# Linear attention and a four-expert block: neighbouring chunks share up products

## The chip, the cores and the metric

The kernel runs on one core of one Trainium2 chip. A core has five engines that work side by side: TensorE (matrix multiplication, "PE" in the profile, its weight loads "PEld"), VectorE ("DVE"), ScalarE ("ACT"), GpSimd ("POOL") and SyncE ("SP", which here only issues DMAs). TensorE writes to the PSUM banks; DVE and ACT carry results from there to SBUF. The metric is the device time of one execution in microseconds (us), the median of several runs.

## The reference

Two blocks follow each other. The first is a linear attention: for each of 8 batches and 8 heads (576 tokens, head size 64) it forms `kv = k^T v`, multiplies `q` by it, and divides every row of 64 numbers by its root mean square. Joined over the heads that gives `x` with 4608 rows of 512 numbers. The second block sends every row through all four experts and adds the results:

```python
kv = np.einsum('bhsd,bhse->bhde', k, v)
out = np.einsum('bhsd,bhde->bhse', q, kv)
x = out / sqrt(mean(out*out, -1) + 1e-6) * g_norm      # -> (4608, 512)
p = domain_probs / (domain_probs.sum(-1, keepdims=True) + 1e-09)
for e in range(4):
    out += p[:, e:e+1] * (np.maximum(x @ w1[e], 0.0) @ w2[e])   # w1: 512x1024, w2: 1024x512
```

Everything is float32.

## The kernel before, in words

**Chunks and steps.** The rows of `x` are cut into 9 chunks of 512 tokens: one for each batch (its first 512 tokens), and a ninth made of the 64 left-over tokens of all 8 batches. A step is one chunk through one expert: expert 0 takes all nine chunks, then expert 1, and so on, 36 steps in all. During expert 0 the attention of the next batch runs beside the products of the current chunk. `CHUNKS` (L2117) holds the order of the chunks in each expert; in expert 1, chunk 0 comes fifth.

**Seven products for eight, twice.** The product `x @ w1[e]` ("up") and the product `h @ w2[e]` ("down") are not done as plain blocks. A product of 2 x 2 blocks is done with seven block products in place of eight (Strassen's scheme in Winograd's form), at the price of additions of blocks. This is done at two levels: seven outer products, numbered 1 to 7 in the code (`OUTER`), each of which is again done as seven inner products (`ORDER`). So "up" has 49 inner products for a chunk. An inner product multiplies a 128 x 256 piece of the weights with 128 tokens; it is issued as four matmul calls (`halves_of`, L585, two halves of 64 columns for each of two pieces of 128 units), and the profile shows eight matmul instructions for each: the weights are stationary, 128 tokens move through. The weights' forms are made once for an expert, the tokens' forms once for a chunk; expert 0 writes the latter to DRAM (`keep`, `x_kept`), and later experts read them back (`x_again`, L1476) into five buffers of kind `xf`, one for each outer product, 512 KB each.

**Up, `up` (L1514).** The inner products of one outer product go to three PSUM banks. Products 1, 6, 7 and 4 add up in the first one; after product 1, ACT copies the bank into the second bank as a seed (L1563, `u<-u`), on which product 2 adds; products 5 and 3 add up in the third. After products 6 and 7, ACT copies the state of the first bank to a small SBUF buffer (`snap`). Two of the four quarters of the result are ACT copies of a bank (L1563, `big<-u`), and two are DVE additions of a bank and a `snap` (L1571). So one outer product costs five ACT passes and two DVE passes over 128 x 256 numbers. Then the outer results are added up (`combine`, L608, on DVE or POOL), and ACT applies the ReLU (L1527).

**Down, `down_deep` (L1819).** Its seven outer products are done in groups of up to two. The results are added in SBUF (L1944); ACT multiplies them by the token's probability into two accumulator buffers of the kind `big` (`result`, L1681; `merge`, L1716), and `send` (L1732) sends them out: in expert 0 as plain stores by SP, in later experts as adding DMAs by POOL (L1740), 128 rows of 2 KB in one DMA. The last step adds in SBUF instead. The first seven chunks of expert 0 use `down_first`, in which three products are done in one level with 256 moving numbers.

**Norm's factors.** For each batch of expert 0 the sums of squares come from TensorE; ACT and DVE make the inverse roots, SP stores them in a small DRAM tile `roots` (L1297) and reads them back spread over the partitions (`spread` L1303, `spread_left` L1311), in rows of 512 and 128 bytes; DVE multiplies (L1322).

**What sets the order.** Nothing is ordered by hand. Every operation is given to a planner (`class Plan`, L44) with a key (its place in steps), a cost on each engine that may do it, its reads and its writes. The planner plays the execution and gives each engine a fixed order, picking the operation with the earliest due time among those that are ready, or for SP the first by key. It also gives out the buffers. `DEALS` (L72) lists for some steps numbers of random draws that shift due times there.

Of the kernel before, what the change touches and what calls it, by code (L numbers as in the profile page):

```python
# [43 lines left out]
class Plan:  # L44
# [25 lines left out]
    FIRST = "SP",  # L70
    BLOCK, ASKED, BEGUN, IDLE, FULL = 256, 30, 66, 20, 45.0
    DEALS = {  # L72
# [4 lines left out]
    }  # L77
    SHARED, AHEAD, INORDER = ("big",), 0.3, ("xf",)

# [375 lines left out]
def kernel(  # L455
# [65 lines left out]

    BANKS = {"u1": 2, "u2": 2, "db": 2, "ab": 2}
    SHAPE = {
        "big": (31, 2 * NT), "w1y": (7, 768), "xa": (1, 4 * NT), "xb": (1, 4 * NT),
        "w2e": (1, 2 * NT), "snap": (5, HN),
        "ss": (2, H), "rt": (2, 2 * H),
    }
    slots = {
# [5 lines left out]
    for kind, n in BANKS.items():  # L534
# [14 lines left out]
    slots["small"] = [small_home[:, 2 * QW:2 * QW + NT]]  # L549
    slots["small2"] = [small_home[:, 2 * QW + NT:2 * QW + 3 * NT]]  # L550
    slots["w2y"] = [w2y_home[:, i, :] for i in range(3)]
    halved = slots["db"]
# [3 lines left out]
    later = [  # L556
        ((kind,), "xf", [slots[kind][0][:, i * 2 * NT:(i + 1) * 2 * NT] for i in range(n)])
        for kind, n in (("xa", 2), ("xb", 2), ("w2e", 1))
    ] + [
        (("raw",), "db", halved),  # L560
        (("kv", "kvbd"), "w2y", [kv_flat[:, i * 768:(i + 1) * 768] for i in range(4)]),
# [8 lines left out]
        for c in range(NCH) for m in ("h0", "h1", 1, 2, 3, 4, 5, 6, 7)  # L570
    }
    roots = {
        b: dram.tile([D, P + 32], F32, tag=f"roots{b}", name=f"roots{b}") for b in range(1, B)
    }

    plan = Plan()
# [544 lines left out]
    def attention(b, key, span, rem):  # L1121
# [160 lines left out]
        def invert(eng):  # L1282
# [11 lines left out]
        sent, kept_roots = Buf(None, f"root{b}"), roots[b]  # L1294
        plan.add(
            when, SPC,
            lambda eng: nc.sync.dma_start(out=kept_roots[:], in_=both[0].ap[0:P:2, 0:wide]),  # L1297
            reads=both[:1], writes=[sent], kb=41, lands=2.6,
        )
        for s, (qt, tokens, mine) in enumerate(done):  # L1300
            xh = x_halves(b)[s]

            def spread(eng, xh=xh, s=s):  # L1303
                rows = kept_roots[:].rearrange("(n i s r) t -> r s i n t", i=2, s=2, r=2)
                for r in range(2):
                    nc.sync.dma_start(
                        out=xh.ap[r * D:(r + 1) * D, :].rearrange("p (n t) -> p n t", t=P),
                        in_=rows[r, s, 0, :, 0:P].unsqueeze(0).to_broadcast([D, 8, P]))

            def spread_left(eng, s=s, mine=mine):  # L1310
                rows = kept_roots[:].rearrange("(j i s r) t -> r s i j t", i=4, s=2, r=2)  # L1311
                for r in range(2):
                    nc.sync.dma_start(
                        out=xs.ap[r * D:(r + 1) * D, mine].rearrange("p (j t) -> p j t", j=NR),
                        in_=rows[r, s, 0, :, P:wide].unsqueeze(0).to_broadcast([D, NR, R]))
# [4 lines left out]
            plan.add(  # L1320
                when, dve(2 * NT),
                lambda eng, xh=xh, qt=qt: nc.vector.scalar_tensor_tensor(  # L1322
                    out=two(xh.ap[:]), in0=tokens(qt.ap, False), scalar=gcol[:], in1=two(xh.ap[:]),
                    op0=ALU.mult, op1=ALU.mult),
                reads=[qt, xh], writes=[xh], port=True,
            )
# [149 lines left out]
    def x_again(c, key, step):  # L1476
        views = {}
        for j, m in enumerate(OUTER):
            f = Buf("xf", f"xl{c}_{m}")
            if m in (1, 2, 3):  # L1480
                half = "h0" if m == 1 else "h1"
                cols = slice(HN if m == 3 else 0, NT if m == 3 else HN)
                load(
                    key + j * step, f, lambda f=f: two(f.ap[:, 0:NT]),
                    two(x_kept[c, half][:])[:, :, cols], 256, reads=[kept[c, half]],
                )
                load(
                    key + j * step, f, lambda f=f: f.ap[:, NT:], x_kept[c, m][:], 256,
                    reads=[kept[c, m]],
                )  # L1490
            else:
                load(
                    key + j * step, f, lambda f=f: f.ap[:], x_kept[c, m][:], 512,
                    reads=[kept[c, m]],
                )
            views[m] = {
                n: (f, lambda f=f, at=at: f.ap[:, at * P:(at + 1) * P])
                for n, at in ((1, 0), (2, 2), (3, 3), (5, 4), (7, 5), (6, 6), (4, 7))
            }
        return views  # L1500


    hidden = {}
    summed = {}
# [9 lines left out]
    def up(s, e, views):  # L1514
# [16 lines left out]
        for i, m in enumerate(OUTER):  # L1531
# [64 lines left out]
            if m == 2:  # L1596
                add(key, unit(1), made[1], made[2])
                relu(key, h[1])
            elif m == 6:
                add(key, made[1], made[1], made[6])  # L1600
            elif m == 5:
                add(key, made[6], made[1], made[5])
            elif m == 3:
                add(key, unit(21), made[6], made[3])
                relu(key, h[21])
                add(key, unit(7), h[1], h[21], ALU.subtract)
            elif m == 7:
                add(key, made[1], made[1], made[7])
                add(key, unit(4), made[1], made[5], where=dve)
                relu(key, h[4])  # L1610
                add(key, unit(5), h[21], h[4], where=dve)
                add(key, unit(6), h[5], h[1], ALU.subtract, dve)
            elif m == 4:
                add(key, unit(2), made[1], made[4])
                relu(key, h[2])
                add(key, unit(3), h[2], h[6], ALU.subtract)
        hidden[s] = h

    def up_plain(s, e, c, key, span):
# [199 lines left out]
    def down_deep(s, e, c, groups=((1, 6), (7, 5), (4, 2), (3,)), base=None, h=None, merge=None, send=None, ends=False, sink=None):  # L1819

        mixed = h is not None
        if not mixed:
            h = hidden.pop(s)
            base = s + 1.2
            merge, send = result(s, e, c, base)
        prods, half = {}, {}

        for i, group in enumerate(groups):
# [132 lines left out]
            elif mixed:  # L1964
                out_(3, 0, 1)
                if not ends:
                    out_(5, 0, 1)
                    out_(5, 1, 1)
                    send(key, 2)
                    send(key, 3)  # L1970
                    send(key, 0)
                    send(key, 1)
            elif i == 0:
                add(6, 1, 6)
            elif i == 1:
                add(7, 6, 7)
                add(6, 6, 5)
                add(5, 7, 5)
                out_(5, 1, 1)
            elif i == 2:  # L1980
                add(4, 7, 4)
                out_(4, 1, 0)
                send(key, 2)
                send(key, 3)
                add(2, 1, 2)
                out_(2, 0, 0)
            else:
                add(3, 6, 3)
                out_(3, 0, 1)
                send(key, 0)  # L1990
                send(key, 1)

    def down_first(s, e, c):

# [119 lines left out]
    inner = {0: weights_2(0, 0.25, 0.04, 8.2)}  # L2114
    inner[0]((1, 7, 6, 5), 0.5)
    norm_probs(0.10)
    CHUNKS = {e: list(range(NCH)) for e in range(E)}  # L2117
    CHUNKS[1].insert(4, CHUNKS[1].pop(0))
    CHUNKS[E - 1][-2:] = NCH - 1, NCH - 2
    for e in range(E):  # L2120
        for i in range(NCH):
# [7 lines left out]
            if s + 1 < E * NCH:  # L2129
# [3 lines left out]
                    x_views[s + 1] = x_forms(c + 1, s + 0.7)  # L2133
                else:
                    again = CHUNKS[(s + 1) // NCH][(s + 1) % NCH]
                    made = x_first if (s + 1) // NCH == 1 and again == 0 else x_again
                    x_views[s + 1] = made(again, s + (0.05 if e else 0.6), 0.13)
            if s:
# [73 lines left out]
```

## Time and profile before

| | before |
|---|---|
| median of 3 runs | 1631.18 us (1630.81 to 1631.45) |
| the profiled execution's own time | 1631.92 us |
| its span, first to last instruction | 1630.1 us |
| PE busy | 1622.5 us (100%) |
| DVE / ACT / POOL busy | 1337.2 / 986.9 / 612.9 us |
| matmul instructions | 29082 |
| clock granted to TensorE | 1.000 of full speed |

The span lies inside the time of the execution; the rest is start and end. "Busy" is the time in which an engine had at least one instruction in hand. For matmuls, which follow each other in a pipeline, it says little about speed; the distance between the starts of successive instructions says more. Under "idle before", a group of instructions has the time that its engine stood idle ahead of them, and what ended it.

### The profile page before, as it was taken

The numbers are of one execution on the slowest core, as the hardware profiler recorded it, in microseconds if no ns is written. First come the engines' busy times: TensorE is split into PE (matmuls) and PEld (weight loads), VectorE is DVE, ScalarE is ACT, GpSimd is POOL, SyncE is SP. The second block draws the span as 40 slices with busy tenths as digits, with TensorE's granted clock in tenths as the row PEclk, the third lists the DMA queues.
The fourth block names the chain that finished last, engine by engine and source line by source line (L and its number), as shares of the span: only waits on it lengthen the run. The fifth ranks groups of instructions, "written<-read, shape, count | busy, mean of one in ns | idle before, by whom it ended". The sixth has DMA issues, their size and how long they took to land.

```text
span 1630.1 us, 66925 instructions
## 1 busy us (share of the span) xinstructions
PE 1622.5 (100%) x29082; PEld 1564.6 (96%) x29082; DVE 1337.2 (82%) x2188; ACT 986.9 (61%) x2504; POOL 612.9 (38%) x597
## 2 busy tenths in 40 slices
PE   9999999999999999999999999999999999999999
PEld 5788999989999999999999999999999999999998
DVE  5788888889888888878988888887788987777776
ACT  4456655665566666666666666666566666566563
POOL 4233432323443443344344533332344443332232
PEclk9999999999999999999999999999999999999999
DMA  9877787855664435444676454444478544444442
GB/s 242 217 190 204 204 216 194 213 166 205 183 176 125 118 93 156 119 111 113 175 190 144 107 133 114 108 111 111 131 183 184 131 107 117 118 107 117 118 106 53
DMA packets 229312, 241.02 MB, mean 148 GB/s; under 512 B 101047, under 2 KB 172542, under 8 KB 229018
## 3 DMA queue, kind: packets, MB, share of 16 engines
q1 hardware_dynamic: 205402, 199.96, 40.9%
q0 software_dynamic: 23616, 36.78, 15.2%
q8 instruction: 228, 3.74, 1.0%
q14 instruction: 66, 0.54, 0.1%
HBM read 162.21 MB, written 74.47 MB: 145 GB/s over the span
## 4 chain that ended last, share of the span: by engine, by line
PE 98%; DVE 1%; DMA 1%; ACT 0%; issue 0%; SPq 0%; DVEq 0%; ACTq 0%
PE u L585 48%; PE db L585 31%; PE ab L585 16%; PE ab L1193 1%; PE ab L1218 0%; PE ab L1261 0%; PE ab L2156 0%; PE db L1218 0%; DVE big L608 0%; DMA kv<-in_v_dram 0%; DMA out_dram<-big 0%; SPq L2079 0%; PE u L997 0%; DMA small<-in_q_dram 0%; DVE small L608 0%
## 5 line engine op out<-in xcount | busy, mean ns | idle before, releaser
L608 DVE TENSOR_TENSOR big<-big,big 128x1024 f32<-128x1024 f32 (+1 forms) x612 | 547.6, 913 | 32.3 <-ACT big L1527 14.1
L585 PE MATMUL db<-big,big 128*64 128x128 f32 (+1 forms) x5464 | 397.1, 283 | 0.3 <-DVE big L608 0.3
L585 PEld LDWEIGHTS db<-big,big 128*64 128x64 f32 x5464 | 319.1, 137 | 16.7 <-issue 0.6
L1563 ACT ACTIVATE snap<-u 128x256 f32<-128x256 f32 x490 | 187.7, 383 | 178.3 <-PE u L585 156.5
L1571 DVE TENSOR_TENSOR big<-u,snap 128x256 f32<-128x256 f32 x450 | 189.0, 421 | 112.8 <-PE u L585 74.2
L608 POOL TENSOR_TENSOR big<-big,big 128x256 f32<-128x256 f32 (+1 forms) x149 | 165.4, 1111 | 229.6 <-DVE big L608 91.0
L1563 ACT ACTIVATE big<-u 128x256 f32<-128x256 f32 x450 | 172.8, 385 | 84.1 <-PE u L585 63.5
L585 PE MATMUL u<-xb,big 128*64 128x128 f32 x2880 | 212.4, 273 | 0.1
L585 PE MATMUL u<-xa,big 128*64 128x128 f32 x2784 | 205.2, 273 | 0.1
L608 POOL TENSOR_TENSOR big<-big 128x512 f32<-128x512 f32 (+1 forms) x94 | 111.4, 1186 | 235.7 <-DVE big L608 137.4
L1905 ACT ACTIVATE snap<-db 128x256 f32<-128x256 f32 (+1 forms) x268 | 95.3, 356 | 126.8 <-PE db L585 104.4
L585 PEld LDWEIGHTS u<-xb,big 128*64 128x64 f32 x2880 | 168.8, 137 | 2.2 <-issue 0.3
L585 PE MATMUL u<-xa,w1y 128*64 128x128 f32 x2232 | 165.8, 273 | 0.0
L585 PEld LDWEIGHTS u<-xa,big 128*64 128x64 f32 x2784 | 162.5, 137 | 2.2 <-issue 1.2
L585 PE MATMUL u<-xb,w1y 128*64 128x128 f32 x2208 | 164.2, 273 | 0.0
L1527 ACT ACTIVATE big<-big 128x1024 f32<-128x1024 f32 x133 | 139.9, 1054 | 11.0 <-DVE big L608 9.4
L1913 DVE TENSOR_TENSOR big<-ab,snap 128x256 f32<-128x256 f32 x186 | 78.4, 421 | 65.6 <-ACT snap L1905 39.0
L608 DVE TENSOR_TENSOR big<-big 128x512 f32<-128x512 f32 (+1 forms) x167 | 125.2, 756 | 7.6 <-POOL big L608 4.4
L585 PEld LDWEIGHTS u<-xa,w1y 128*64 128x64 f32 x2232 | 130.6, 137 | 0.7 <-DVE xb L608 0.4
L585 PEld LDWEIGHTS u<-xb,w1y 128*64 128x64 f32 x2208 | 129.1, 137 | 1.3 <-issue 0.4
L1740 POOL DMA_DIRECT2D out_dram<-big x124 | 108.0, 1155 | 32.5 <-ACT big L1716 18.0
L1563 ACT ACTIVATE u<-u 128x256 f32<-128x256 f32 x245 | 90.9, 371 | 38.7 <-PE u L585 28.1
(246 smaller groups left out, 2838.8 us busy)
## 6 DMA issues: line engine op xcount, KB each, us to landing
xb<-x SPq DMA_DIRECT2D x44, 512.0 KB, 3.6
xa<-x SPq DMA_DIRECT2D x40, 512.0 KB, 3.6
out_dram<-big POOLq DMA_DIRECT2D x76, 256.0 KB, 6.0
big<-in_moe_w_dram SPq DMA_DIRECT2D x27, 512.0 KB, 6.3
w2e<-x SPq DMA_DIRECT2D x20, 512.0 KB, 3.6
xa<-x_h SPq DMA_DIRECT2D x37, 256.0 KB, 3.5
x_h<-big SPq DMA_DIRECT2D x18, 512.0 KB, 4.9
x<-xb SPq DMA_DIRECT2D x18, 512.0 KB, 4.9
```

Of the source, the lines that this page charges most:

```text
L585: nc.tensor.matmul(out_[cols], lhsT=lhsT[:, cols], rhs=rhs, **kw)
L608: lambda eng: adder(eng).tensor_tensor(out=out_(), in0=a(), in1=b(), op=op),
L1193: nc.tensor.matmul(bank.ap[o * D:(o + 1) * D, r * D:(r + 1) * D], lhsT=ks[r], rhs=vs[r], start=(j == r == 0), stop=(j == len(sets[0]) - 1) ...
L1527: lambda eng: nc.scalar.activation(out=b.ap[:], in_=b.ap[:], func=ACT.Relu),
L1563: lambda eng: nc.scalar.activation(out=where(), in_=ps.ap[:, 0:HN], func=ACT.Copy),
L1571: lambda eng: nc.vector.tensor_tensor(out=block(whole, a, t), in0=src.ap[:, 0:HN], in1=add_.ap[:], op=ALU.add),
L1740: nc.gpsimd.dma_start(out=dst, in_=cell(i)[parts, :], accum_op=ALU.add)
L1905: lambda eng: nc.scalar.activation(out=where(), in_=group_of(ps.ap), func=ACT.Copy),
L1913: lambda eng: nc.vector.tensor_tensor(out=cell(tq, dq), in0=group_of(src.ap), in1=group_of(add_.ap), op=ALU.add,),
```

## The change

**Joint up products.** In experts 1 to 3, `up_shared` takes the place of `up`. Neighbouring chunks of an expert share three of their seven outer products, in turn 6, 7, 4 and 2, 3, 5: an inner product of those is issued once with 256 moving tokens, 128 of each chunk. Chunk 0 in expert 1 has no partner. `course` gives every outer product its place; 8 pairs of neighbours in experts 2 and 3 and 6 in expert 1 make 22 pairs. The five `xf` buffers become one tile (`x_home`), so that two of them can be read by one access pattern of two runs of 128; a joint outer product holds two of them, and `x_again` loads them at keys that `course` gives. A bank of a joint product holds 512 numbers for each partition. There is no seed: ACT copies the bank after products 1, 6 and 7 straight to the place of a result quarter, for each chunk, and DVE adds to that in place after products 2, 5 with 7, and 3. For each chunk of a joint outer product that makes four ACT passes and three DVE passes. Single outer products are evacuated as before. The ReLU and several sums are made in place.

**Down finished in place.** `down_whole` takes the place of the form of `down_deep` with accumulators (steps 7 to 34): ACT multiplies the results where they lie (`finish`), and each of the four results of 256 tokens x 256 columns is sent on its own, in rows of 1 KB. The groups of outer products alternate with the chunk (`DEEP`).

**Norm's factors.** The inverse roots are stored by two DMAs into two DRAM tiles, and read back by one DMA each in place of two, in rows of 4 KB and 512 bytes.

**Draws.** `DEALS` lists other draws, and for 35 of the 39 steps from -3 to 35; before for 21.

```diff
-        -3: (920, 388), -2: (494, 764), -1: (959, 295), 0: (983,), 3: (1126, 364), 4: (981, 960), 5:
...
+        -3: (920, 388), -2: (494, 764, 638), -1: (959, 295, 323), 0: (1187,), 1: (859,), 2: (321,),
...
+    x_home = pool.tile([P, 5, 2 * NT], F32, tag="x", name="x")
+    x_at = [x_home[:, i, :] for i in range(5)]
...
+    HEADS, ENDS = (2, 3, 5), (6, 7, 4)
+    MIDDLES = (1,), (1,)
+    DEEP = ((1, 6), (7, 5), (4, 2), (3,)), ((4, 5), (2, 1), (7, 6), (3,))
...
-            plan.add(when, {"SP": 1.2}, spread, reads=[sent], writes=[xh], kb=520, lands=6.2)
-            plan.add(when, {"SP": 1.28}, spread_left, reads=[sent], parts=[xs], kb=100, lands=6.0)
+            def spread(eng, i, to, s=s):
+                rows = roots[b][i][2 * s:2 * s + 2].rearrange("r n t -> r (n t)")
+                return nc.sync.dma_start(out=to, in_=rows.unsqueeze(1).to_broadcast([2, D, rows.shape[1]]))
...
+    def course(e):
+        uses, at, shared = [{} for _ in range(NCH)], 0.0, ()
+        for i, c in enumerate(CHUNKS[e]):
+            turn = i % 2
+            first, end = (ENDS, HEADS) if turn else (HEADS, ENDS)
+            beside = i + 1 < NCH and not (e == 1 and 0 in (c, CHUNKS[e][i + 1]))
...
+            for m in joint:
+                uses[i][m] = uses[i + 1][m] = at, 2
+                at += 2
...
+    def up_shared(s, e, i, uses, views, following):
...
+                    if n == 1:
+                        x = both[0][m][mm][1]()
+                    else:
+                        lo, hi = sorted(place(0)[0])
+                        col = both[0][m][mm][2] * P
+                        x = x_home[:, lo:hi + 1:hi - lo, col:col + P]
+                    for u in range(2):
+                        halves_of(
+                            ps.ap[:, u * n * P:(u + 1) * n * P], w[:, u * P:(u + 1) * P], rhs=x,
+                            start=((mm in (1, 5) or mm == 2 and n == 2) and u == 0), stop=True,
+                            skip_group_check=True,
+                        )
...
+                if joint:
+                    for o in range(2):
+                        if mm in (1, 6, 7):
+                            early(o, *{1: (0, 0), 6: (0, 1), 7: (1, 1)}[mm])
+                        if mm == 2:
+                            total(o, 0, 0, ps, None)
+                        elif mm == 7:
+                            total(o, 1, 1, bank[5], None)
+                        elif mm == 4:
+                            copy(o, wholes[o], lambda o=o, cell=cell: cell(o, 1, 0))
+                        elif mm == 3:
+                            total(o, 0, 1, ps, None)
+                    continue
...
+    def finish(s, e, c, q, th, dh, key, prods, half, whole):
...
+                    out=whole(q)[:, t * HN:(t + 1) * HN], in_=whole(q)[:, t * HN:(t + 1) * HN],
+                    func=ACT.Copy, scale=p_all[:, c * NR + i, e:e + 1]),
...
+    def down_whole(s, e, c, turn):
...
+                for parts, b, dst in where:
+                    src = two(whole(q))[parts, b, :]
+                    if e:
+                        nc.gpsimd.dma_start(out=dst, in_=src, accum_op=ALU.add)
+                    else:
+                        nc.sync.dma_start(out=dst, in_=src)
...
+            if e:
+                up_shared(s, e, i, uses[e], x_views.pop(s), x_views.get(s + 1))
             elif s:
                 up(s, e, x_views.pop(s))
...
-                down_deep(s, e, c)
+                down_whole(s, e, c, i % 2 if e else 0)
```

More of the change, by code (lines that the diff above doesn't have):

```diff
@@ L556 @@
     later = [
[L557 to L558 removed]
+        ((kind,), "xf", x_at[at:at + n]) for kind, at, n in (("xa", 0, 2), ("xb", 2, 2), ("w2e", 4, 1))
     ] + [
@@ L572 @@
     roots = {
-        b: dram.tile([D, P + 32], F32, tag=f"roots{b}", name=f"roots{b}") for b in range(1, B)
+        b: [
+            dram.tile([n, D // n, width], F32, tag=f"roots{b}_{n}", name=f"roots{b}_{n}")
+            for n, width in ((8, P), (16, 32))
+        ] for b in range(1, B)
     }
@@ L1293, in attention @@
             when, {"DVE": 0.57 + 0.0031 * wide}, invert, reads=[ss, both[0]], writes=both[:1], port=True)
[L1294 to L1299, printed above, removed]
+        sent = [Buf(None, f"root{b}_{i}") for i in range(2)]
+        for i, cols in enumerate((slice(0, P), slice(P, wide))):
+            plan.add(
+                when, SPC,
+                lambda eng, i=i, cols=cols: nc.sync.dma_start(
+                    out=roots[b][i][:].rearrange("m n t -> n m t"), in_=both[0].ap[0:P:2, cols]),
+                reads=both[:1], writes=[sent[i]], kb=(32, 8)[i], lands=2.6,
+            )
@@ L1500, in x_again @@
         return views
+    def course(e):
[4 more added lines that the diff above has]
+            beside = i + 1 < NCH and not (e == 1 and 0 in (c, CHUNKS[e][i + 1]))
+            todo = [m for m in OUTER if m not in shared] if not turn and not shared else [
+                m for m in first + MIDDLES[turn] + end if m not in shared]
+            joint = end[::-1] if turn else end
+            joint = joint if beside else ()
+            for m in todo:
+                if m not in joint:
+                    uses[i][m] = at, 1
+                    at += 1
+            for m in joint:
+                uses[i][m] = uses[i + 1][m] = at, 2
+                at += 2
+            shared = joint
+        return uses
     hidden = {}
@@ L1817, in down, with down_deep @@
             down_deep(s, e, c, ((4, 2), (3, 5)), base + 3 / 7, h, merge, send)
[L1819 to L1828, printed above, removed]
+    def down_deep(s, e, c, groups, base, h, merge=None, send=None, ends=False, sink=None, full=False):
+        mixed = not full
         prods, half = {}, {}
@@ L1978, in down_deep @@
                 add(5, 7, 5)
-                out_(5, 1, 1)
-            elif i == 2:
+                emit(5, 1, 1, key, prods, half, whole)
                 add(4, 7, 4)
[L1982 to L1991, printed above, removed]
+                emit(4, 1, 0, key, prods, half, whole)
+            elif i == 3:
+                add(1, 6, 3)
+                emit(1, 0, 1, key, prods, half, whole)
+        down_deep(s, e, c, groups, base, h, sink=sink, full=True)
+        for i, b in now.items():
+            summed[c, i] = b
     def down_first(s, e, c):
```

262 lines of the change are left out of this document (235 added, 27 removed), and 8 rows, old and new, of the table DEALS.

## The prediction

> **What bounds the kernel now.** I read the page first, then the busy times by stage, then the waits.
>
> ```profile
> span 1630.1 us, 66925 instructions
> PE 1622.5 (100%) x29082; PEld 1564.6 (96%) x29082; DVE 1337.2 (82%) x2188; ACT 986.9 (61%) x2504; POOL 612.9 (38%) x597
> PE 98%; DVE 1%; DMA 1%; ACT 0%; issue 0%; SPq 0%; DVEq 0%; ACTq 0%
> ```
>
> ```profile
> 20.00:470.00 450.00, 448.04 (x7642) 396.56 (x7642) 374.35 (x626) 262.76 (x671) 159.33 (x145) 1.00 0.71 195
> 470.00:860.00 390.00, 390.00 (x7142) 389.43 (x7140) 334.95 (x534) 245.87 (x617) 161.42 (x162) 1.00 0.55 140
> 860.00:1240.00 380.00, 380.00 (x6968) 380.00 (x6964) 317.07 (x506) 237.51 (x602) 147.29 (x143) 1.00 0.51 128
> 1240.00:1600.00 360.00, 360.00 (x6600) 359.90 (x6597) 284.62 (x459) 222.96 (x565) 131.14 (x125) 1.00 0.48 116
> ```
>
> The columns are the stretch, its length, the busy time of PE, PEld, DVE, ACT and POOL with instruction counts, the granted clock, the DMA share and GB/s. The chain of work that ended last is PE for 98%. The four stretches are about experts 0, 1, 2 and 3. A busy PE proves little, so I use the counts: 380.00 / 6968 = 54.5 ns for each matmul instruction in the third stretch, 360.00 / 6600 = 54.5 in the fourth, 390.00 / 7142 = 54.6 in the second. Is that the pace of back-to-back work? The timeline of PE says yes:
>
> ```profile
> 679.81 1.04 PE L585 MATMUL db<-w2y,big 128*64 128x128 f32 x16
> ...
> 699.46 0.61 PE L585 MATMUL u<-xa,big 128*64 128x128 f32 x8
> ```
>
> Between these two starts lie 360 instructions of 128 moving rows, the 16 of the first row among them: 19.65 us / 360 = 54.6 ns, or 0.4367 us for an inner product of eight. So experts 1 to 3 hold no stall that could be won back. There only fewer or cheaper matmuls shorten the run. All waits of PE that the profile names add up to 3.5 us:
>
> ```profile
> PE u L585 <- DMA small<-in_q_dram: 1.2, 1, 1.2
> PE ab L2156 <- DVE eps L2163: 1.0, 1, 1.0
> PE ab L1063 <- DVE big L928: 0.8, 1, 0.8
> PE db L585 <- DVE big L608: 0.3, 1, 0.3
> PE ab L1193 <- DMA out_dram<-big: 0.2, 1, 0.2
> ```
>
> **Joint products on PE.** 22 pairs of chunks x 3 outer x 7 inner products = 462 joint products, each eight instructions of 256 moving rows for sixteen of 128: 3696 matmuls fewer. Up in experts 1 to 3 has no 256-row matmul before; the nearest rows are those of the last step, with contiguous operands:
>
> ```profile
> 1610.98 1.90 PE L585 MATMUL u<-big,big 128*64 128x256 f32 x16
> 1612.70 1.04 PE L585 MATMUL db<-big,big 128*64 128x128 f32 x16
> ...
> 1614.89 1.90 PE L585 MATMUL u<-big,big 128*64 128x256 f32 x16
> 1616.61 0.61 PE L585 MATMUL db<-w2y,big 128*64 128x128 f32 x8
> ...
> 1618.36 1.90 PE L585 MATMUL db<-big,big 128*64 128x256 f32 x16
> 1620.09 0.61 PE L585 MATMUL db<-small,big 128*64 128x128 f32 x8
> ```
>
> From start to next start sixteen take 1.72, 1.72 and 1.73 us, so eight take 5.17 / 6 = 0.862 us. Two products of 128 rows take 2 x 0.4367 = 0.873. The gain is 0.011 us for a joint product; with two digits in each time it may be 0.008 to 0.015. The other bound is a longer stretch of 512-row matmuls at the start:
>
> ```profile
> 25.92 8.80 PE L585 MATMUL u<-big,big 128*64 128x512 f32 x40
> 34.65 1.14 PE L1085 MATMUL db<-kv,big 64*64 64x64 f32 x16
> ```
>
> That is 8.73 / 40 = 218 ns, exactly four times 54.6: by this row longer matmuls win nothing. It ends in a change of tile shape, which the joint products don't have, so I take 0.010, the lower side of the nearer rows. 462 x 0.010 = **-4.6 us**; the ends are 0 and 462 x 0.015 = -6.9. The moving operand now has two runs in two buffers, which no row shows; a price for it is what the end at 0 stands for.
>
> The Trainium skill ("TensorE: Matmul & The Clock Gate", section "Wait — 56ns, not 53.3ns?") gives each warm matmul its rows at 2.4 GHz and about 2.5 ns that don't depend on the rows. By it a joint product would save 8 x 2.5 = 20 ns, 9.2 us in all, an estimate from that page. The trace disagrees: its 54.5 ns lie under the 55.8 that the rule gives for 128 rows, so half the fixed cost at most is there to be saved.
>
> **What evacuates the joint products.** For each chunk of a joint outer product one ACT pass goes and one DVE pass comes.
>
> ```profile
> L1571 DVE TENSOR_TENSOR big<-u,snap 128x256 f32<-128x256 f32 x450 | 189.0, 421 | 112.8 <-PE u L585 74.2
> L1563 ACT ACTIVATE u<-u 128x256 f32<-128x256 f32 x245 | 90.9, 371 | 38.7 <-PE u L585 28.1
> ```
>
> 22 x 3 x 2 = 132 passes: DVE +132 x 0.421 = 55.6 us, ACT -132 x 0.371 = -49.0 us. By expert DVE gets 36, 48 and 48 passes, 15.2, 20.2 and 20.2 us: 335 + 15 of 390 is 90%, 317 + 20 of 380 is 89%, 285 + 20 of 360 is 85%. The largest idle time ahead of L1571 is time spent waiting for PE, so DVE runs ahead of its input there. The chain inside a bank relaxes for PE: before, product 6 waited for one ACT pass of 371 ns against a product of 437; now it waits for two passes, some 0.75 us, against a product of 0.862, with the down products of the step before between them as now. Cost on the path: 0, hidden under PE; if that cover goes, up to the whole 55.6, which is the slower rival below. ReLUs and sums keep their number and sizes.
>
> **x loads.** Their number stays; their places on SP move, and a joint product frees its two buffers together.
>
> ```profile
> SPq L614 <- PE u L585: 916.3, 192, 10.7
> xb<-x SPq DMA_DIRECT2D x44, 512.0 KB, 3.6
> ```
>
> SP already spends 916 us standing before a load until PE frees a buffer; behind it wait the next loads, the next expert's weights and the stores. A step has 49 up and 49 down products, 98 x 0.4367 = 42.8 us, and a joint outer product takes two sevenths of it, 12.2 us. The two loads that its end releases, even one after the other, take 7.2 us and are wanted when the next joint product is through. So they land 5 us early: 0. Without that cover each would cost PE what it is late.
>
> **Down in place.** ACT's eight scalings in a step stay at the same price (501 and 503 ns, below). Sends by POOL: 128 before; after, chunks 1 to 7 have 4, chunk 0 has 8, chunk 8 has 16, so 52 x 3 less the last step's 4 = 152.
>
> ```profile
> L1716 ACT ACTIVATE big<-big,p_all 128x256 f32<-128x256 f32 x196 | 91.1, 501 | 2.0 <-DVE big L1944 1.0 <-POOL big L1944 0.7
> L2024 ACT ACTIVATE big<-big,p_all 128x256 f32<-128x256 f32 x56 | 26.2, 503 | 9.5 <-DVE big L2059 6.3 <-DVE big L1944 2.6 <-POOL big L1944 0.4
> L1740 POOL DMA_DIRECT2D out_dram<-big x124 | 108.0, 1155 | 32.5 <-ACT big L1716 18.0
> L719 POOL DMA_DIRECT2D big<-in_moe_w_dram x17 | 22.0, 1295 | 17.1 <-ACT snap L1563 11.7 <-issue 2.7 <-ACT big L1563 1.6
> out_dram<-big POOLq DMA_DIRECT2D x76, 256.0 KB, 6.0
> ```
>
> 24 x 1.155 = 28 us more on POOL, and up to 1.295 each if shorter rows cost as much as the 512 KB weight sends (152 x 0.14 = 21 us more). POOL is busy 38%, and nobody waits for a landing of 6 us but the same rows' send nine steps later: 0 on the path. If POOL's slack were gone, its additions would go to DVE. Two buffers of kind `big` come free in a step, and three results of the next chunk take their place for longer: 0, either way unshown.
>
> **Norm's factors and the draws, expert 0.**
>
> ```profile
> L1306 SPq DMA_DIRECT2D big<-roots x28: 573/627/2007, 56.7 to 352.2; - x28
> L1313 SPq DMA_DIRECT2D snap<-roots x28: 573/607/770, 58.1 to 353.6; - x28
> L1297 SPq DMA_DIRECT2D roots<-big x7: 482/494/508, 54.8 to 346.3; - x7
> DVE big L1322 <- DMA big<-roots: 2.4, 2, 1.6
> ```
>
> For each of 7 batches four issues of 0.62 us go and one of 0.49 comes: SP loses 7 x 2.0 = 14 us, and 28 x 512 fewer packets of 512 bytes become 14 x 128 of 4 KB. The wait that this could end is DVE's, 2.4 us in all; PE waits nowhere for `roots`, since it works on the chunk before. So 0 from that alone. The new order can remove PE's waits in this stretch (1.2 + 0.3 + 0.2 = 1.7 us) or make two new ones like the 1.2: -1.7 to +2.4. I take **-0.4**, a quarter of the first, as the transfers that PE waits for there meet fewer packets.
>
> **Sum.** -4.6 - 0.4 = -5.0 on 1631.92, the profiled execution's own time (span 1630.1 and 1.8 around it): 1626.9. That execution lies 0.7 above the median of the runs, 1631.18; so for a median **1626.2 us**.
>
> **The rivals.** A. *DVE keeps full banks occupied.* Place: the readings of a joint bank that product 6, or the next outer product, needs empty. DVE works in a fixed order, among additions of 1024 numbers:
>
> ```profile
> L608 DVE TENSOR_TENSOR big<-big,big 128x1024 f32<-128x1024 f32 x300 | 398.4, 1331 | 25.7 <-ACT big L1527 14.1 <-PE db L585 1.6 <-DMA big<-in_moe_w_dram 1.0
> ```
>
> It is in such an addition 398.4 / 1630.1 = 24% of the time, with 0.67 us still to go on average: 0.16 us of delay for each of the 132 added passes, 21 us in all where PE has nothing else to do. At half of it uncovered the change costs 10.7 - 5.0 = +5.7: **1636.9**. From 23% uncovered the gain is gone. For it: DVE at 90% on average is full in places. Against it: the 74.2 us that DVE waits for PE ahead of just these passes. The Trainium skill ("TensorEngine Tiling (Array Packing)", section "PSUM Bottleneck") warns that a faster array doesn't empty PSUM faster; before, no wait of PE for an evacuation stands in the trace.
>
> B. *Two runs cost what longer rows save*, so joint products win nothing and the change doesn't do on PE what it says: 1631.2 - 0.4 = **1630.8**. For it the 512-row stretch, against it the three 256-row ones.
>
> C. *Expert 0 gives half back*: the joint products bring 4.6, two new waits cost 2.4: **1629.0**. For it: all of PE's waits for transfers lie there, and the order of its steps is drawn anew. Against: SP and the DMA engines have less to do.
>
> D. *The part of a matmul that doesn't depend on its rows is twice what the three rows say*: 0.022 us for a joint product, 462 x 0.022 = 10.2, and 0.4: **1620.6**. The three readings exclude it unless two runs of rows pass quicker than one. The skill's rule above points this way.
>
> **How the numbers follow.** Forecast 0.60, A 0.15, B 0.12, C 0.10, D 0.03. A measurement of this kernel can tell about 0.2%, 3.3 us: below 1627.9 is faster, above 1634.4 slower. The forecast and D are faster, 0.63; B and C within, 0.22; A slower, 0.15. The forecast's own range is 1622.6 (both gains at their ends, 6.9 + 1.7) to 1627.9. The range reaches on to 1633.0, past B and C and to A's lighter forms (30% uncovered gives 1632.6); A itself and D, 0.18, are left out.
>
> **What would show it.** Right: 29082 - 3696 = 25386 matmuls, with 3696 of 256 rows into `u`; eight of them 0.862 to 0.866 us apart; in each of experts 1 to 3 PE without waits, and each shorter by 1.3 to 1.7 us (126, 168 and 168 joint products x 0.010); DVE 85 to 90% busy there. A shows as waits of PE for DVE or ACT behind `u` banks, B as eight instructions 0.873 us apart, C as waits for DMA in the first 470 us, later than 1.2 us. The prediction is wrong in its core if PE's instruction pace in experts 1 to 3 is right and the time isn't, or if DMA sends of 1 KB rows turn up in a wait of PE.

## The result, and the profile after

The changed kernel takes 1744.82 us (median of 4 runs, 1744.19 to 1745.67), the kernel before on the same chip 1631.32 (1630.81 to 1631.77). The ratio is 1.0696, with a 95% interval of 1.0678 to 1.0715: 7% slower, 113.5 us, where 1626.2 was forecast.

The page of the changed kernel: span, busy times, PE and its granted clock in 40 slices, the chain of work that ended last by engine, and one group of instructions.

```profile
span 1742.6 us, 59130 instructions
PE 1646.8 (95%) x25386; PEld 1451.3 (83%) x25386; DVE 1344.8 (77%) x2302; ACT 915.1 (53%) x2372; POOL 710.5 (41%) x639
PE   9796798797799999999999999999999999999998
PEclk9898998898899999999999999999999999999999
PE 85%; DMA 10%; DVE 3%; ACT 1%; issue 1%; SPq 0%; DVEq 0%; ACTq 0%
L1329 DVE SCALAR_TENSOR_TENSOR big<-small,gcol,big 128x1024 f32<-128x1024 f32 x14 | 18.0, 1284 | 111.0 <-DMA big<-roots 111.0
```

The 25386 matmuls and ACT's 132 passes fewer are those that were foretold; DVE has 114 instructions more and not 132, and POOL 42 more: 24 DMA issues and 18 additions, which the planner gave to POOL in place of DVE. But PE is no longer 98% of the chain. DMA has 10% of it, and among the first eleven of the 40 slices, in expert 0, most have holes in PE's row and in its clock's. The last line says whose they are: the fourteen multiplications by norm's factors waited 111.0 us for the reading of `roots`.

The stages of the two kernels tell how much of the loss lies there (columns as in the prediction; the first stretch of before is shown there).

```profile
20.00:470.00 450.00, 362.72 (x5688) 309.67 (x5688) 276.02 (x461) 193.80 (x501) 118.81 (x106) 0.89 0.54 149
860.00:1240.00 380.00, 380.00 (x5664) 331.47 (x5662) 318.04 (x553) 214.24 (x558) 180.58 (x154) 1.00 0.55 132
```

In the same 450 us PE gets 5688 matmuls done and not 7642. At the 450.00 / 7642 = 58.9 ns that one took before, the 1954 that are missing make 115 us: about the whole loss, and it lies in expert 0. The later stretch is as full as before. The 112.5 us between the spans are made of three parts. PE stands idle 1742.6 - 1646.8 = 95.8 us, 88.2 more than before. It is busy 1646.8 us where run 1 below, with the same matmuls in the same order, is busy 1619.2: 27.6 us go into a lower pace. And run 1's 1619.2 are 3.3 less than before: 88.2 + 27.6 - 3.3 = 112.5.

PE's waits, then DVE's first one:

```profile
PE u L593 <- DVE big L1596: 49.4, 9, 15.4
PE u L593 <- DVE big L1329: 38.8, 6, 8.3
```

```profile
DVE big L1329 <- DMA big<-roots: 111.0, 14, 10.2
```

The second row, 38.8 us, goes straight back to the multiplication by the factors (L1329), which makes the next chunk's `x`. The first row, 49.4 us, is for L1596, an evacuation of a `u` bank that needs no factors at all. The timeline shows why it is late (start, duration, instruction, idle time before it and what ended it):

```profile
251.26 18.42 SPq L1318 DMA_DIRECT2D snap<-roots  x2
...
256.87 1.90 PE L593 MATMUL db<-big,big 128*64 128x256 f32 x16
...
262.79 1.28 DVE L1329 SCALAR_TENSOR_TENSOR big<-small,gcol,big 128x1024 f32<-128x1024 f32 x1 [7.05 <-DMA big<-roots]
264.00 0.42 DVE L1596 TENSOR_TENSOR big<-u,snap 128x256 f32<-128x256 f32 x1
...
264.47 1.12 PE L593 MATMUL u<-x,w1y 128*64 128x128 f32 x8 [5.71 <-DVE big L1596]
```

DVE's order is fixed, and L1596 stands behind L1329. SP stands 18.42 us at two issues, DVE waits 7.05 us for the factors and turns to the bank 1.21 us after it has begun with them, and PE, out of banks, has waited 5.71 us. So both lines of PE's waits have one cause. What it is, the chain of waits shows (start, us to landing):

```profile
59.57 22.08 DMA big<-roots
130.03 23.89 DMA big<-roots
190.39 24.18 DMA big<-roots
250.69 22.15 DMA big<-roots
315.85 22.08 DMA big<-roots
381.27 21.89 DMA big<-roots
447.07 22.29 DMA big<-roots
```

and the rows of the line that issues these DMAs (shortest, median and longest issue in ns, first and last start):

```profile
L1318 SPq DMA_DIRECT2D big<-roots x14: 516/543/8148, 58.9 to 447.1; - x14
L1318 SPq DMA_DIRECT2D snap<-roots x14: 550/8056/10196, 60.1 to 455.8; - x14
```

The second reading of each of the seven batches lands 22 to 24 us after its issue. The issues beside it hold SP for 8 us where 0.6 was the rule before. And the DMA engines are not full meanwhile; the stretch behind the first of these issues:

```profile
62.00:80.00 18.00, 8.39 (x114) 7.29 (x108) 3.57 (x11) 2.27 (x6) 2.14 (x3) 0.74 0.13 52
```

A DMA share of 0.13 is 0.13 x 16 = 2.1 of the 16 engines: as much work as two engines can do. The view doesn't tell the engines apart; that the work lies on just two is tested below.

### The profile page after: what moved, and what is told of

Its sections match the earlier page's. It is cut to its first block, busy times and chain, and to the rows that moved or that the text cites. A ratio compares the mean times of both kernels' runs of the same rounds, so it can differ in the third digit from the quotient of the medians.

```text
span 1742.6 us, 59130 instructions
## 1 busy us (share of the span) xinstructions
PE 1646.8 (95%) x25386; PEld 1451.3 (83%) x25386; DVE 1344.8 (77%) x2302; ACT 915.1 (53%) x2372; POOL 710.5 (41%) x639
## 4 chain that ended last, share of the span: by engine, by line
PE 85%; DMA 10%; DVE 3%; ACT 1%; issue 1%; SPq 0%; DVEq 0%; ACTq 0%
PE u L593 42%; PE db L593 26%; PE ab L593 15%; DMA big<-roots 9%; DVE big L616 1%; PE ab L1204 1%; DVE big L1329 0%; PE ab L1229 0%; PE ab L2456 0%; DMA roots<-big 0%; DMA kv<-in_k_dram 0%; DMA kv<-in_v_dram 0%; PE ab L1272 0%; SPq L622 0%; PE db L1229 0%
## 5 line engine op out<-in xcount | busy, mean ns | idle before, releaser
L616 DVE TENSOR_TENSOR big<-big,big 128x1024 f32<-128x1024 f32 (+1 forms) x548 | 495.8, 921 | 27.0 <-POOL big L616 11.9
L593 PE MATMUL u<-x,big 128*64 128x128 f32 (+1 forms) x4800 | 454.2, 319 | 0.2 <-ACT snap L1588 0.2
L593 PE MATMUL u<-x,w1y 128*64 128x128 f32 (+1 forms) x3720 | 365.1, 321 | 49.3 <-DVE big L1596 49.1
L593 PE MATMUL db<-big,big 128*64 128x128 f32 (+1 forms) x5632 | 409.9, 285 | 0.1
L593 PEld LDWEIGHTS db<-big,big 128*64 128x64 f32 x5632 | 336.4, 138 | 36.8 <-issue 1.0
L593 PEld LDWEIGHTS u<-x,big 128*64 128x64 f32 x4800 | 304.3, 138 | 52.7 <-ACT snap L1588 0.8
L593 PEld LDWEIGHTS u<-x,w1y 128*64 128x64 f32 x3720 | 236.9, 139 | 94.7 <-DVE big L1596 51.2
L1792 DVE TENSOR_TENSOR big<-u,big 128x256 f32<-128x256 f32 x369 | 141.5, 417 | 46.6 <-PE u L593 31.2
L593 PE MATMUL ab<-w2y,big 128*64 128x128 f32 x1544 | 110.3, 278 | 0.0
L1329 DVE SCALAR_TENSOR_TENSOR big<-small,gcol,big 128x1024 f32<-128x1024 f32 x14 | 18.0, 1284 | 111.0 <-DMA big<-roots 111.0
L593 PE MATMUL u<-big,big 128*64 128x128 f32 (+2 forms) x544 | 66.4, 375 | 38.8 <-DVE big L1329 38.8
L2192 ACT ACTIVATE big<-big,p_all 128x256 f32<-128x256 f32 x200 | 96.0, 507 | 8.6 <-POOL big L2156 6.0
L593 PE MATMUL ab<-big,big 128*64 128x128 f32 x1456 | 99.1, 273 | 0.0
L593 PEld LDWEIGHTS ab<-w2y,big 128*64 128x64 f32 x1544 | 92.4, 140 | 2.2
```

Of the source, the lines that this page charges most:

```text
L593: nc.tensor.matmul(out_[cols], lhsT=lhsT[:, cols], rhs=rhs, **kw)
L616: lambda eng: adder(eng).tensor_tensor(out=out_(), in0=a(), in1=b(), op=op),
L1329: lambda eng, xh=xh, qt=qt: nc.vector.scalar_tensor_tensor(out=two(xh.ap[:]), in0=tokens(qt.ap, False), scalar=gcol[:], in1=two(xh.ap[:]), ...
L1792: lambda eng: nc.vector.tensor_tensor(out=cell(o, a, t), in0=rows(o, src), in1=own[0].ap[:].rearrange("p (u t) -> p u t", t=P) if own else ...
L2192: lambda eng, t=t, i=2 * th + t: nc.scalar.activation(out=whole(q)[:, t * HN:(t + 1) * HN], in_=whole(q)[:, t * HN:(t + 1) * HN], func=ACT ...
```

## The experiments

My theory after this profile: the reading has its two factor rows as the slowest index, with 64 copies of each behind it, and for that reason runs on two DMA engines. Before, the 64 copies were the slowest index. Rivals: the 4 KB rows are slow in themselves; or the other parts of the change (joint products, down in place, the order) hold DVE and PE up and the reading is late as a consequence.

**1. One DMA for each row.** Same order, same rows of 4 KB, same bytes; only the slowest index is now the 64 copies.

```diff
-                rows = roots[b][i][2 * s:2 * s + 2].rearrange("r n t -> r (n t)")
-                return nc.sync.dma_start(out=to, in_=rows.unsqueeze(1).to_broadcast([2, D, rows.shape[1]]))
+                for r in range(2):
+                    row = roots[b][i][2 * s + r:2 * s + r + 1].rearrange("r n t -> r (n t)")
+                    nc.sync.dma_start(
+                        out=to[r * D:(r + 1) * D], in_=row.to_broadcast([D, row.shape[1]]))
```

> The changed kernel with the same plan and the same 4 KB rows, but the factors of a batch are read back by two DMAs for each half, one for each of its two rows, so that 64 copies of a row, not two rows, are the slowest index. Theory T (a DMA whose slowest index has two values runs on two of the 16 DMA engines): 256 packets of 4 KB at 0.165 us over 16 engines are 2.6 us in place of 21, DVE waits less than 5 us for the factors in all, PE less than 4 us for anything, and the time is that of the forecast, 1631.3 - 4.6 = 1626.7 (1624 to 1630). Rival S (rows of 4 KB, or 64 reads of one DRAM address, are slow in themselves): landing stays near 20 us and the time at 1735 to 1745. Rival O (the new order of expert 0 or the loads of the joint products make the stalls): 1735 to 1745 too.

1630.01 us (1628.62 to 1631.57), before beside it 1630.86; ratio 0.9995 (0.9986 to 1.0005). The loss is gone, at the price of twice the issues. The time lies at the upper end of the 1624 to 1630 expected, 3.3 us above the 1626.7 named. Its page:

```profile
span 1627.0 us, 59186 instructions
PE 1619.2 (100%) x25386; PEld 1427.7 (88%) x25386; DVE 1346.1 (83%) x2302; ACT 915.2 (56%) x2372; POOL 711.6 (44%) x639
```

The issues of the line, DVE's wait for what they read (us, times), and the stage of expert 0:

```profile
L1319 SPq DMA_DIRECT2D big<-roots x28: 444/559/1272, 58.1 to 349.6; - x28
...
  DVE big L1331: 2.5, 5
```

```profile
20.00:470.00 450.00, 448.93 (x7646) 397.04 (x7647) 375.06 (x614) 262.07 (x668) 168.19 (x154) 1.00 0.71 197
```

7646 matmuls in the first 450 us, four more than before the change, at the full clock, with issues of 0.56 us. DVE waits 2.5 us for the factors and not 111.0. The 4 KB rows are not slow in themselves: that rival is out. So is the new order as the cause, since run 1 keeps it.

**2. Each factor row stored twice** (by one more store for each batch, not shown), so that one DMA reads four rows of 4 KB with 32 copies each. The 512-byte rows are read as in the changed kernel.

```diff
...
-                rows = roots[b][i][2 * s:2 * s + 2].rearrange("r n t -> r (n t)")
-                return nc.sync.dma_start(out=to, in_=rows.unsqueeze(1).to_broadcast([2, D, rows.shape[1]]))
+                n = 2 if i else 4
+                rows = roots[b][i][n * s:n * s + n].rearrange("r n t -> r (n t)")
+                return nc.sync.dma_start(
+                    out=to, in_=rows.unsqueeze(1).to_broadcast([n, P // n, rows.shape[1]]))
```

> The changed kernel with every row of factors stored twice side by side, so that one DMA reads four rows of 4 KB, 32 copies each, for a half: the slowest index has four values. One more store of 32 KB for each batch (0.6 us of SP). T: four engines, 256 x 0.165 / 4 = 10.6 us for both halves in place of 21; the stall of PE in a batch falls from 113.5 / 7 = 16 us to about 6, and the time to about 1626.7 + 7 x 6 = 1669 (1650 to 1690). S with slow rows: 1740 to 1750, unchanged. O: unchanged.

1678.43 us (one run), between the changed kernel and run 1, inside the 1650 to 1690 expected. Two rows of its chain, its first stretch, and DVE's wait:

```profile
62.29 11.95 DMA big<-roots
...
335.16 11.89 DMA big<-roots
```

```profile
62.00:74.00 12.00, 7.80 (x124) 6.75 (x120) 4.16 (x12) 2.65 (x7) 2.14 (x3) 0.91 0.23 91
```

```profile
DVE big L1334 <- DMA big<-roots: 48.8, 14, 4.9
```

With four rows the same bytes land in 11.9 to 15.0 us over the seven batches instead of 21.9 to 24.2, and the share is 0.23 x 16 = 3.7 engines. For two rows and for four, the number of rows in the slowest index is the number of engines' worth of work that the share shows. Taken as 128 packets on each of two engines in 22.08 us and 64 on each of four in 11.95, a packet of 4 KB takes (22.08 - 11.95) / 64 = 0.16 us, an estimate.

**3. Only the new reading, in the kernel before.** The new form of norm's factors with nothing else of the change; the order is planned anew, with before's draws. The two tiles and their stores are not shown.

```diff
...
-            plan.add(when, {"SP": 1.2}, spread, reads=[sent], writes=[xh], kb=520, lands=6.2)
-            plan.add(when, {"SP": 1.28}, spread_left, reads=[sent], parts=[xs], kb=100, lands=6.0)
+            plan.add(
+                when, SPC, lambda eng, xh=xh, spread=spread: spread(eng, 0, xh.ap[:, :]),
+                reads=sent[:1], writes=[xh], kb=520, lands=5.0)
```

> The kernel before with the new reading of the norm's factors alone (two tiles, one DMA of two rows for each half, the planner's new costs for it); no joint products, accumulators and draws as before. T: the loss comes with it alone, 1631.3 + 100 to 120 = 1731 to 1751. O: 1631, within 3 us.

1759.85 us (one run), 129 above before. Its waits of PE:

```profile
PE u L588 <- DVE big L1321: 56.1, 7, 14.0
PE u L588 <- DVE big L1570: 21.7, 5, 7.5
```

The same two lines (L1321 is the multiplication by the factors, L1570 the evacuation behind it). The reading alone makes the whole loss and needs no joint product beside it. It came out 9 us above the upper end of what was expected; runs 4 and 6 show what may have added them: here, too, draws made for one set of operations order another.

**4. Everything but the new reading.** The changed kernel with the factors read as before; planned anew, with the changed kernel's draws.

```diff
-            def spread(eng, i, to, s=s):
-                rows = roots[b][i][2 * s:2 * s + 2].rearrange("r n t -> r (n t)")
...
+            plan.add(when, {"SP": 1.2}, spread, reads=[sent], writes=[xh], kb=520, lands=6.2)
+            plan.add(when, {"SP": 1.28}, spread_left, reads=[sent], parts=[xs], kb=100, lands=6.0)
```

> The changed kernel with the norm's factors as before (rows of 512 bytes, 64 copies slowest), planned anew with the draws of the changed kernel. T: 1626.7, up to 3 more since the draws were made for another plan: 1625 to 1630. O: 1735 to 1745. Against the run with two issues: the difference is what 4 KB rows are worth when they are spread over the engines; I expect 0 to 2 us.

1646.14 us (1645.05 to 1648.9), ratio 1.0095 (1.0080 to 1.0110): a miss by 16 us. Nearly all of the loss goes with the reading, but something else costs 1%. Its PE has only small waits (the longest 1.0 us) at full clock, but many of them. What differs from run 1, beside the reading, is the order: draws that were searched for one set of operations were applied to another.

**5. Joint products split again.** Run 1 with each joint product issued as two of 128 rows; order, buffers and evacuations unchanged.

```diff
-                        halves_of(
-                            ps.ap[:, u * n * P:(u + 1) * n * P], w[:, u * P:(u + 1) * P], rhs=x,
...
+                        for o in range(n):
+                            halves_of(
+                                ps.ap[:, (u * n + o) * P:(u * n + o + 1) * P],
+                                w[:, u * P:(u + 1) * P], rhs=x[:, o] if n == 2 else x,
```

> The kernel of the run with two issues, with the same order on every engine, but every joint product issued as two sets of 128 moving rows, one after the other, in place of one of 256; loads, banks and evacuation stay joint. It measures the joint products by themselves. The forecast's price (0.010 us each, 462 of them): 4.5 us slower than with two issues (1630.0), 1634.5 (1633 to 1636), with 29082 matmuls. Rival B (two runs of 128 cost what longer rows save): 1630, within 1 us. Rival A (evacuation sets PE's pace): 1630 too, since PE would wait for the same readings.

1634.95 us (1633.34 to 1636.28) beside a before of 1630.68; ratio 1.0026 (1.0016 to 1.0036). So the joint products bring 1634.95 - 1630.01 = 4.9 us (5.1 if each is first set against the before beside it). They do what they were to do. And with PE's work as before the change, the rest of the change (its order, evacuations, loads and sends together) is 4.3 us slower than the kernel before.

**6. Run 1 with the draws of before**, to test what unsuited draws cost.

```diff
-        -3: (920, 388), -2: (494, 764, 638), -1: (959, 295, 323), 0: (1187,), 1: (859,), 2: (321,),
...
+        -3: (920, 388), -2: (494, 764), -1: (959, 295), 0: (983,), 3: (1126, 364), 4: (981, 960), 5:
```

> The kernel of the run with two issues, planned with the draws of the kernel before; nothing else differs. The run with the old factors was 16 us slower than the one with two issues, although both read the factors quickly. If that was the order that unsuited draws give, this run loses as much: 1640 to 1655, with PE's lost time spread over expert 0 and the later experts. If it was the old way of reading the factors, this run stays at 1630, within 3 us.

1651.86 us (1651.30 to 1652.81), ratio 1.0129 (1.0114 to 1.0145): 22 us for the draws alone. The waits of PE are as in run 4, many and small, the largest row being

```profile
PE u L591 <- ACT big L1782: 3.9, 7, 1.3
```

So the 16 us of run 4 are of the size that unsuited draws make. That they are its cause was not shown by itself.

**7 and 8. New draws.** Run 7 is run 1 with draws chosen for just this kernel; the planner also reckons the two issues at 1.15 us of SP now. Run 8 has, beside its own draws, the old form of down with accumulators and 128 sends of 2 KB rows. The first lines shown are run 7's, the last run 8's.

```diff
-        -3: (920, 388), -2: (494, 764, 638), -1: (959, 295, 323), 0: (1187,), 1: (859,), 2: (321,),
...
+        -2: (35, 17), 0: (353, 212), 1: (394,), 2: (879, 391), 3: (694, 1062), 4: (822,
...
-        groups = DEEP[turn]
-        was = {i: summed.get((c, i)) for i in range(NR)}
-        now = {i: Buf(None, f"o{s}_{i}") for i in range(NR)}
+        merge, send = result(s, e, c, base)
```

> The changed kernel with each factor row read by its own DMA (64 copies slowest), and the order planned anew with draws chosen for just this kernel. The work of PE is that of the run with two issues, 25386 matmuls, of which 462 x 8 have 256 rows; against before that is 462 x 9.7 ns = 4.5 us less. The run with two issues and the changed kernel's order ended 0.85 us below before, and its profile lost 0.7 us more than before's in the last step and 0.7 us between the last matmul and the end. Theory 1: these losses belong to the order, so another order can avoid part of them: 1626.5 to 1629.0. Theory 2: they belong to down in place, which sends the last chunks in more and smaller pieces whatever the order: 1629.0 to 1631.0, no difference from the run with two issues.

> As the run before it, but down as before the change: with accumulators of 128 rows and 128 sends by POOL in rows of 2 KB in place of 152 in rows of 1 KB, draws chosen for this kernel too. Theory 1 (down in place costs nothing on the path, and the losses at the end belong to the order): within 1 us of the run before it. Theory 2 (down in place costs the 1.4 us at the end): 1 to 2 us below the run before it, with the last matmul 4.0 us before the end as before the change and not 4.7. It would be slower than that run by more than 1 us if the buffers that down in place sets free were worth something on the path, which I had put at 0.

Beside a before of 1631.06 (1629.96 to 1632.86), run 7 takes 1629.39 (1628.48 to 1630.53), ratio 0.9989 (0.9980 to 0.9997), and run 8 1629.20 (1627.88 to 1629.79), ratio 0.9988 (0.9979 to 0.9997). Both are faster than the kernel before (by 0.1%) and than the changed one; 0.1% is less than the 0.2% that was said to be told from nothing, but with eleven runs of each beside 21 of the kernel before the intervals just exclude no change. They are 0.2 us apart: down in place, each form with its own draws, neither wins nor costs anything that shows, as forecast. On run 7 alone the second theory's range held; run 8, within 1 us of it, speaks against that theory, since the accumulators bring nothing. The rows of DVE's last pass, of before, run 1, run 7 and run 8 in turn, say the same of the end:

```profile
1626.45 0.61 DVE L1724 SCALAR_TENSOR_TENSOR big<-ab,p_all,big 128x128 f32<-128x128 f32 x2 [0.26 <-PE ab L585]
```

```profile
1622.62 0.61 DVE L1942 SCALAR_TENSOR_TENSOR big<-ab,p_all,big 128x128 f32<-128x128 f32 x2 [0.26 <-PE ab L593]
```

```profile
1623.89 0.61 DVE L1941 SCALAR_TENSOR_TENSOR big<-ab,p_all,big 128x128 f32<-128x128 f32 x2 [0.26 <-PE ab L592]
```

```profile
1622.51 0.61 DVE L1941 SCALAR_TENSOR_TENSOR big<-ab,p_all,big 128x128 f32<-128x128 f32 x2 [0.26 <-PE ab L592]
```

From there to the end of the spans (1630.1, 1627.0, 1627.6 and 1626.7) it is 3.7, 4.4, 3.7 and 4.2 us. The longer end of run 1 is not down in place's own, since run 7 has it short and run 8 has it longer again.

## Why the prediction was wrong

**Norm's factors: the step that failed.** The prediction said: "PE waits nowhere for `roots`, since it works on the chunk before. So 0 from that alone." It counted packets ("28 x 512 fewer packets of 512 bytes become 14 x 128 of 4 KB") and SP's issues, and took "less to do" for sooner done. It didn't ask over how many engines a DMA's packets are dealt. Nor does PE work on the chunk before all the time: the row `PE u L593 <- DVE big L1329: 38.8, 6, 8.3` is six waits for the new chunk itself. The rows it quoted had the place but not that size: `DVE big L1322 <- DMA big<-roots: 2.4, 2, 1.6` showed that in two cases of fourteen DVE already came before the factors, so there was little cover. A reading landed after a median of 4.9 us before; now the last one of a batch lands 22 us after its issue. Over seven batches that is (22 - 5) x 7 = 119 us later, and DVE waited 111.0 of them: by this estimate the cover was about 1 us for a batch.

The Trainium skill states the rule, in "DMA: Bandwidth & Descriptors", section "Why a DMA increments its semaphore by 16 and not by 1": the largest number up to 16 that divides the slowest dimension of both access patterns is the number of engines used. Its section "Rules for kernel authors" adds that an outermost dimension of c < 16 confines the whole DMA to at most c engines. The trace agrees, with shares of 2.1 and 3.7 of 16 engines for two and four rows. This was the rule that spoke against the change, and the prediction didn't weigh it.

**The range for expert 0** ("-1.7 to +2.4") was made from PE's waits of before, priced at 1.2 us each. It could not hold a wait that PE had never had. What was missing is the chain behind it: DVE in a fixed order holds an evacuation that needs no factors, and PE runs out of banks. Of the lost time 88.2 us are PE standing still and 27.6 us a lower pace, which I hadn't counted either:

```profile
142.78 1.12 PE L593 MATMUL u<-big,big 128*64 128x128 f32 x8 [7.42 <-DVE big L1329]
143.69 1.92 PE L593 MATMUL ab<-w2y,big 128*64 128x128 f32 x16
145.39 0.71 PE L593 MATMUL u<-big,big 128*64 128x128 f32 x8
145.93 0.60 PE L593 MATMUL db<-w2y,big 128*64 128x128 f32 x8
146.37 0.60 PE L593 MATMUL db<-x,big 128*64 128x128 f32 x8
```

After 7.42 us of idleness sixteen instructions take 145.39 - 143.69 = 1.70 us, twice the 0.87 of full pace; full pace is back after some 3 us, so one such wait costs about 1.5 us beyond itself. The Trainium skill ("TensorE: Matmul & The Clock Gate", section "Part 1: The HAM clock gate (the "warmup" mystery)") gives half the clock after an idle window of about 3.4 us until as long a busy one, and the trace agrees.

**Joint products: right.** -4.6 was forecast, 4.9 to 5.1 measured by splitting them (run 5). The timeline of the changed kernel gives their pace:

```profile
866.22 1.03 PE L593 MATMUL u<-x,big 128*64 128x256 f32 x8
867.08 1.03 PE L593 MATMUL u<-x,w1y 128*64 128x256 f32 x8
867.95 3.20 PE L593 MATMUL u<-x,big 128*64 128x256 f32 x32
```

From 866.22 to 867.95 sixteen instructions take 1.73 us, 0.865 for eight, within the 0.862 to 0.866 that were to show it. (The third row merges two shapes; only its start is used.)

**Evacuations, x loads: right** on the path. From 472 us on no wait of PE is longer than 0.4 us, with DVE busy 318.04 / 380 = 84% in the stretch shown, just under the 85 to 90% foretold. The price beside the path was off: DVE's busy time grew by 7.6 us and not by 55.6, while POOL's grew by 97.6, since the planner moved additions there. **Down in place: right** on the path (run 8). POOL's sends cost 24 more issues, and those below took 1.529 us each, where 1.295 was the bound:

```profile
L2230 POOL DMA_DIRECT2D out_dram<-big x138 | 147.4, 1529 | 83.0 <-ACT big L2192 27.3 <-issue 13.6 <-ACT snap L2117 10.5
```

**The rivals.** A's sign, waits of PE for DVE behind `u` banks, did appear, but in expert 0, which has no joint products, and from a DVE that stood waiting, not from one that was full; in run 1 only 0.4 us of it is left. D (a larger fixed part) did not come, B (two runs cost what longer rows save) falls with run 5. C had the place, expert 0 waiting for transfers, but with a price of 2.4 us where 115 were lost.

**The sum without the failed step.** With the reading mended (run 1) the kernel gains 0.85 us by the medians, an interval that includes none, where 5.0 were forecast. 4.9 come from the joint products, so the rest of the change gives 4 back, and draws suited to it (run 7) return 0.8 of these: 1.7 in all. These 0.8 lie inside the intervals of the two runs. The draws were put at -1.7 to +2.4 for expert 0 alone; run 6 shows that they can cost 22. Where the other 3 us lie stays open: no row of waits is large enough to name them, and executions of one kernel differ by 3 us (run 1).

## What to carry to other kernels

Before a DMA is merged, look at the slowest index of both its access patterns: fewer and longer packets were slower here when that index was 2 (22 us) or 4 (12 to 15 us) and not 64. A transfer priced at 0 because it is hidden must be priced again with its new landing time against the cover that its consumer has, and with everything that stands behind that consumer in a fixed order. An order that was searched for one set of operations is part of that kernel: compare variants under the same order, or search for each.

## What the runs showed that I had not expected

- With two rows as slowest index a DMA keeps about two of the 16 engines at work (share 0.13), and 1 MB takes 22 us; with four rows it is 0.23 and 12 to 15 us.
- Issues of SP behind such a DMA take 8.1 us (median) instead of 0.6: the queue stands still, with all that is behind it.
- An idle time of 7.4 us is followed by some 3 us of PE at half pace; of the 115.6 us between the spans of the changed kernel and run 1, 27.6 are lower pace.
- Draws made for another kernel cost 22 us (1.3%) with no wait of PE over 1.7 us.
